# Weight transfers issued by ScalarE, fewer transfers of v, and one attention level on TensorE for two segments

## The chip, the cores and the metric

The kernel runs on one core of one Trainium2 chip. The metric is the device time in microseconds of one execution; for the kernel before, the median of 3 runs is 972.37 us (972.09 to 973.37). A profile is taken of one further execution.

## What is computed

A gated linear attention over 4 batches, 8 heads, 768 tokens and a head dimension of 48 gives a matrix of 3072 x 384. It goes through two layers of matrix products, one after the other:

```python
f = 1.0 / (1.0 + np.exp(-f_logit))
for t in range(S):
    state = f[:, :, t, :, None] * state + np.einsum('bhd,bhe->bhde', k[:, :, t], v[:, :, t])
    y[:, :, t] = np.einsum('bhd,bhde->bhe', q[:, :, t], state)
x = y.transpose(0, 2, 1, 3).reshape(B * S, H * D)
x = ((x @ w_a) * (x @ w_b)) @ w_out
h = np.maximum(np.maximum(x @ w1, x @ w2), x @ w3)
out = h @ w_out2
```

w_a and w_b are 384 x 1536, w_out 1536 x 384, w1 to w3 384 x 768 and w_out2 768 x 384. The weights arrive as float64.

## The kernel before

The 3072 tokens are cut into 12 segments of 256 tokens, three to a batch. In each segment 128 partitions hold the tokens of 8 heads; within a segment tokens are combined in levels of doubling width.

For a segment, SP loads q, k, f and v (`load_nat`, L182, two transfers each), a second layout of v called `vst` (`load_vst`, L194, 8 transfers), and from it the level operands `vlev` (`load_vlev`: segment 0 straight from `vst`, L207, 28 transfers; later segments by way of DRAM, `store_vscr` L199 and L213, 2 and 12 transfers). `direct_steps` (L229 to L283) does the levels of width 1, 2 and 4 inside blocks of 8 tokens, as elementwise multiplications and reductions: L229 to L232 width 1, L237 to L241 width 2, L248, L260, L276, L281, L282 and L283 width 4. It writes the products of decays `tp` (L257), the keys and queries `kp` and `qp` and the result so far, `op`. `attn_steps` then transposes these on TensorE (L304; ScalarE copies the results from PSUM: `c_tot` L312, `kt` and `qt` L337), builds decay tables on VectorE (L320 to L329), multiplies state and tokens (L366, L394), and does the levels of width 8, 16 and 32 as scores (L407), a mask on VectorE (L412) and a product with `vlev` (L424). `c_out` (L429) copies the segment's result, and SP transfers carry it to `xf` (L440), the input of the first MoE layer.

That layer splits every operand in a high and a low fp32r part, so that each product is three matmuls: x into `xh` (ScalarE L490) and `xl` (VectorE L493), products with w_a and w_b into `pa` and `pb` (L502), their product `a` (L512) split in `gh` (L516) and `gl` (L521), products with w_out (L531). The second layer follows in six blocks of 512 tokens (`up2` L675, `down` L701).

Weights are converted from float64 by integer and float steps in `conv_steps`, 36 units of 128 x 384 for the first layer: two activations on ScalarE (L573, L574), one step on VectorE (L579), one on GpSimd (L583), a cast on ScalarE to the high part (L590), and the low part (L595) on VectorE or GpSimd. SP issues their loads (`load_w1`, L613, and L609 for w_out).

All engines run their instructions in order. The string `ORDER` sets that order: every step is queued under a letter, and each letter of the string takes the next step of that queue. Steps called `flex` run on VectorE unless their number is in `ON_POOL`, which sends them to GpSimd. DMAs take eight completion lanes in turn, and a transfer waits for the one eight before it.

The diff touches all of `ORDER` and `ON_POOL`, the loads, `direct_steps`, `attn_steps`, `conv_steps` and the places of the second layer's buffers.

Of the kernel before, what the change touches and what calls it, by code (L numbers as in the profile page):

```python
# [7 lines left out]
F32 = mybir.dt.float32  # L8
# [35 lines left out]
    "ooGMNouMXNMuMHuoooNuoNMuoMoMuNouoMNooOuMoopOMuONuuXOMNoMouMGXoHoNuMoNMuXMuGuuNooHoNMooMoGuMoNMoXoHoN"
    "uMuMuNoMNuuoMpMGoNuoGMouooOouOYNMMNuXuouMXoNMOMouOouNoMNouMuMooNoHNMuMuoMouooNuuuMoGNHoXMHMooNuuMouX"
    "pNMoMouoNMoOouuGoONMoMOuNuMoHNOuMMGoNooMoooNuHuMMuNuuMoouoNMMuXuooNuXMoGNuXHMMoooNMNuouMXMuoooNMNuuo"
    "ouMOMoNuOouMNoOooMMONouuNMXuoMMXuNMouooNouMMoooNMouooNuMMuNouNMuooMMNooMoXOXoXoOoXOXOX"
# [30 lines left out]
def kernel(  # L78
# [31 lines left out]
    NB2 = NT // TB  # L110
    mm = nc.tensor.matmul
# [3 lines left out]
    vscr = [dram.tile([SEG, 2, 4 * D], F32, name=f"vscr{s}") for s in range(NSEG)]  # L115
# [32 lines left out]
    masks = cst.tile([P, 3, 64], U8, name="masks")  # L148
# [10 lines left out]
    tp = at.tile([P, 2, 64], F32, name="tp")  # L159
    vst = at.tile([P, 2, 2, 4, D], F32, name="vst")  # L160
    vlev = at.tile([P, 3, 2, 4 * D], F32, name="vlev")
    qt = at.tile([P, 128, 8], F32, name="qt")
# [24 lines left out]
    def load_vst(s):  # L187
        b, s0 = s // SPB, (s % SPB) * SEG
        for g in range(2):
            t0 = s0 + g * P  # L190
            for half in range(2):
                for hp in range(2):
                    h0 = 4 * hp + (half ^ hp)
                    sp.dma_start(out=vst[:, g, half, 2 * hp:2 * hp + 2],  # L194
                                 in_=v[b, h0:h0 + 3:2, t0:t0 + P, :].rearrange("h p d -> p h d"))

    def store_vscr(s):
        for g in range(2):
            sp.dma_start(out=vscr[s][g * P:(g + 1) * P], in_=vst[:, g].rearrange("p a h d -> p a (h d)"))  # L199

    def load_vlev(s):
        for lev in range(3):
            w = 8 << lev
            for hl in range(2):
                if s == 0:
                    for x in range(64 // w):
                        sp.dma_start(  # L207
                            out=vlev[64 * hl + x * w:64 * hl + (x + 1) * w, lev],
                            in_=vst[2 * x * w:2 * x * w + w, :, hl].rearrange("p g h d -> p g (h d)"),
                        )  # L210
# [603 lines left out]
```

## Time and profile before

| what | value |
| --- | --- |
| runs, median (lowest to highest) | 972.37 us (972.09 to 973.37) |
| the profiled execution | 973.67 us, span 971.9 us |
| TensorE matmul busy | 905.5 us (93%) |
| VectorE, ScalarE, GpSimd busy | 572.9, 336.1, 305.0 us |
| DMA | 79.07 MB, 81 GB/s in the mean |

The span is the profiled part of that execution; 1.8 us lie around it. TensorE carries the matmuls, VectorE is DVE in the rows, ScalarE ACT, GpSimd POOL, and SPq the DMA queue of SP. A busy share is a mean over stages with different limits; the rows further down are cut by stage.

### The profile page before, as it was taken

To read this page: it belongs to the slowest core of one execution; us is meant where nothing else is said; L and a number is where in the kernel's file an instruction comes from. 1 tells how busy PE (TensorE), PEld (TensorE's weight loads), DVE (VectorE), ACT (ScalarE), POOL (GpSimd) and SP (SyncE) were. 2 spreads that over 40 slices of the span, in tenths; PEclk is the share of its full clock that TensorE was granted. 3 is DMA by queue.
4 is the path that set the end of the run, shared out by engine and by line. 5 is a ranking of instruction groups with operands and counts; after the bars stand their busy time and mean duration, and the time that the engine had idled before them with its cause. 6 is when DMAs were issued, how large, how long until landed. Compare 5 with 4: busy or idle time off the path is not lost.

```text
span 971.9 us, 23339 instructions
## 1 busy us (share of the span) xinstructions
PE 905.5 (93%) x9860; PEld 839.5 (86%) x9860; DVE 572.9 (59%) x893; ACT 336.1 (35%) x640; POOL 305.0 (31%) x297
## 2 busy tenths in 40 slices
PE   1348989999999999999999999999999999999998
PEld 0238879999999999999999999999888888888887
DVE  6989988978886947677865442464522232323221
ACT  3556733423333333242332323564421212112121
POOL 3533737474364336443263300362400000000000
PEclk9998989999999999999999999999999999999999
DMA  8468232334323231133321204261110110010000
GB/s 244 121 198 259 79 98 59 107 76 114 106 70 93 71 115 53 58 95 83 98 84 41 69 9 137 92 212 66 33 37 17 44 49 17 33 34 17 1 32 33
DMA packets 79184, 79.07 MB, mean 81 GB/s; under 512 B 33128, under 2 KB 69864, under 8 KB 79080
## 3 DMA queue, kind: packets, MB, share of 16 engines
q1 hardware_dynamic: 79080, 77.59, 27.1%
q8 instruction: 77, 1.26, 0.5%
q14 instruction: 27, 0.22, 0.1%
HBM read 58.48 MB, written 13.76 MB: 74 GB/s over the span
## 4 chain that ended last, share of the span: by engine, by line
PE 82%; DVE 6%; DMA 6%; SPq 3%; issue 1%; ACT 1%; POOL 0%; DVEq 0%; ACTq 0%
PE p L675 23%; PE pb L502 15%; PE y L531 14%; PE pa L502 14%; PE y L701 4%; DMA ub<-in_moe_w_b_dram 2%; PE pa L701 2%; PE pb L701 2%; DMA kn<-in_k_dram 2%; PE o L424 2%; PE w L304 2%; PE o L394 2%; SPq L440 1%; PE w L407 1%; PE w L366 1%
## 5 line engine op out<-in xcount | busy, mean ns | idle before, releaser
L502 PE MATMUL pa<-xh,ua 128*128 128x256 f32 x864 | 167.7, 290 | 0.0
L502 PE MATMUL pb<-xh,ub 128*128 128x256 f32 x864 | 166.4, 288 | 1.4 <-DVE ub L595 0.9
L531 PE MATMUL y<-gh,uo 128*128 128x256 f32 x864 | 164.7, 286 | 1.5 <-ACT gh L516 0.9
L675 PE MATMUL p<-ub,u 128*128 128x512 f32 x486 | 165.9, 395 | 0.0
L502 PEld LDWEIGHTS pa<-xh,ua 128*128 128x128 f32 x864 | 137.3, 196 | 2.2
L502 PEld LDWEIGHTS pb<-xh,ub 128*128 128x128 f32 x864 | 135.2, 192 | 4.4 <-DVE ub L595 1.3
L531 PEld LDWEIGHTS y<-gh,uo 128*128 128x128 f32 x864 | 135.9, 193 | 3.4 <-ACT gh L516 1.1
L502 PE MATMUL pa<-xl,ua 128*128 128x256 f32 x432 | 124.0, 287 | 2.1 <-DVE xl L493 2.1
L531 PE MATMUL y<-gl,uo 128*128 128x256 f32 x432 | 123.4, 286 | 2.5 <-DVE gl L521 2.5
L502 PE MATMUL pb<-xl,ub 128*128 128x256 f32 x432 | 122.5, 284 | 0.0
L675 PEld LDWEIGHTS p<-ub,u 128*128 128x128 f32 x486 | 90.5, 188 | 19.1
L675 PE MATMUL p<-ua,u 128*128 128x512 f32 x324 | 101.8, 395 | 0.0
L516 ACT CAST gh<-a 128x512 fp32r<-128x512 f32 x72 | 44.6, 620 | 139.9 <-DVE a L512 118.9
L512 DVE TENSOR_TENSOR a<-a,pb 128x512 f32<-128x512 f32 x72 | 49.1, 683 | 73.2 <-PE pb L502 71.4
L502 PEld LDWEIGHTS pa<-xl,ua 128*128 128x128 f32 x432 | 84.4, 195 | 2.8 <-DVE xl L493 2.7
L531 PEld LDWEIGHTS y<-gl,uo 128*128 128x128 f32 x432 | 83.5, 193 | 3.1 <-DVE gl L521 3.1
L685 DVE TENSOR_TENSOR uo<-uo,p 128x512 f32<-128x512 f32 x36 | 24.7, 687 | 101.1 <-PE p L675 84.0
L502 PEld LDWEIGHTS pb<-xl,ub 128*128 128x128 f32 x432 | 83.1, 192 | 0.0
L508 ACT COPY a<-pa 128x512 f32<-128x512 f32 x72 | 42.5, 590 | 88.0 <-DVE gl L521 43.9
L521 DVE TENSOR_TENSOR gl<-a,gh 128x512 fp32r<-128x512 f32 x72 | 64.1, 891 | 12.8 <-ACT gh L516 12.7
L675 PEld LDWEIGHTS p<-ua,u 128*128 128x128 f32 x324 | 60.4, 188 | 11.7
L685 DVE TENSOR_TENSOR ua<-ua,p 128x512 f32<-128x512 f32 x36 | 24.8, 688 | 72.1 <-PE p L675 72.0
(206 smaller groups left out, 1560.0 us busy)
## 6 DMA issues: line engine op xcount, KB each, us to landing
u<-in_moe_w_dram SPq DMA_DIRECT2D x18, 384.0 KB
vlev<-vscr SPq DMA_DIRECT2D x132, 48.0 KB
uo<-in_moe_w_out_dram SPq DMA_DIRECT2D x14, 384.0 KB
qn<-in_q_dram SPq DMA_DIRECT2D x24, 192.0 KB
fn<-in_f_logit_dram SPq DMA_DIRECT2D x24, 192.0 KB
kn<-in_k_dram SPq DMA_DIRECT2D x24, 192.0 KB
ua<-in_moe_w_a_dram SPq DMA_DIRECT2D x12, 384.0 KB
vn<-in_v_dram SPq DMA_DIRECT2D x24, 192.0 KB
```

Of the source, the lines that this page charges most:

```text
L304: mm(pair[0][h], lhsT=pair[1][h], rhs=ident[half(h), half(h)], is_transpose=True, start=first_of_bank(n), stop=True, skip_group_check=True)
L394: mm(os_[0][64 * hl:64 * hl + D, hi // 2, o:o + 64], lhsT=st[64 * hl:64 * hl + D, c, hi * D:hi * D + D], rhs=qv[64 * hl:64 * hl + D, hi, c ...
L424: mm(ov[64 * hl:64 * hl + D, :, 1, :], lhsT=vlev[ps, lev, g, hi * D:hi * D + D], rhs=abs_[g][ps, hi, 64 * lev:64 * lev + 64], start=False, ...
L502: mm(ps, lhsT=col(w, i, j, h), rhs=x2[x][:, i], start=(n == 0), stop=(n == 3 * KC - 1), skip_group_check=True)
L508: act.copy(out=g2[jj][0], in_=ps2["a"])
L512: vec.tensor_mul(out=a, in0=a, in1=ps2["b"])
L516: act.copy(out=g2[jj][1], in_=g2[jj][0])
L521: vec.tensor_sub(out=g2[jj][2], in0=a, in1=gh.bitcast(F32))
L531: mm(ps, lhsT=wts["o", j][:, w, m * P:m * P + P], rhs=g, start=(j == 0 and n == 0 and m != 1), stop=(j == NJ - 1 and n == 2), skip_group_c ...
L675: mm(ps, lhsT=col(n, i, f, w), rhs=y, start=(c == 0), stop=(c == 3 * KC - 1))
L685: vec.tensor_max(out=hset[k][0], in0=hset[k][0], in1=u_ps[b, f, n])
L701: mm(o_ps[t], lhsT=h[:, t * P:t * P + P], rhs=wts[down_units[f]][:, w], start=(f == 0 and n == 0), stop=(f == NF - 1 and n == 2))
```

## The change

All 36 weight loads of the first layer are issued by ScalarE. Three units of one column group share one raw tile and one result tile, and `conv_steps` runs three units through its first three steps before it casts any of them. `vst` comes in 4 transfers instead of 8, goes to DRAM in 3, in all segments, and `vlev` comes in 6. For segments 0 and 1 (`DEEP = 2`) the level of width 4 leaves `direct_steps`: its scores, mask and product become `p_sc4` (L423), `mask4` (L428) and `p_av4` (L440), with two more `vlev` transfers (into a part of `prod`), the two halves of the decays kept apart in `t4`, their product `tt` formed on VectorE (L481), and the keys and queries multiplied by `t4` afterwards (L491, L492). `ORDER` and `ON_POOL` are written anew, and the second layer's buffers are cut from the new groups.

```diff
 def load_vst(s):
-            for half in range(2):
-                for hp in range(2):
-                    h0 = 4 * hp + (half ^ hp)
-                    sp.dma_start(out=vst[:, g, half, 2 * hp:2 * hp + 2],
-                                 in_=v[b, h0:h0 + 3:2, t0:t0 + P, :].rearrange("h p d -> p h d"))
+            for par in range(2):
+                sp.dma_start(out=vst[:, par, g], in_=v[b, par::2, t0:t0 + P, :].rearrange("h p d -> p h d"))
 def store_vscr(s):
-        for g in range(2):
-            sp.dma_start(out=vscr[s][g * P:(g + 1) * P], in_=vst[:, g].rearrange("p a h d -> p a (h d)"))
+        sp.dma_start(out=vscr[s][:, :, :, 0:2 * D].rearrange("p a g x -> p (a g) x"),
+                     in_=vst[:, :, :, 0:2].rearrange("p a g h d -> p (a g) (h d)"))
+        for a in range(2):
+            sp.dma_start(out=vscr[s][:, a, :, 2 * D:4 * D], in_=vst[:, 1 - a, :, 2:4].rearrange("p g h d -> p g (h d)"))
 def load_vlev(s):
-        for lev in range(3):
-            w = 8 << lev
+        for lev in range(-1 if s < DEEP else 0, 3):
+            w = 8 << lev if lev >= 0 else 4
             for hl in range(2):
...
+                sp.dma_start(
+                    out=(vlev[:, lev] if lev >= 0 else vlev4)[64 * hl:64 * hl + 64].rearrange("p g d -> p (g d)"),
+                    in_=vscr[s][:, hl].rearrange("(x two r) g d -> two x r (g d)", two=2, r=w)[0],
+                )
 def direct_steps(s):
-        for h in range(2):
+        for h in range(0 if s < DEEP else 2):
             flex("d", lambda e, h=h: e.tensor_mul(
...
+        if s < DEEP:
+            step("c", lambda: act.copy(out=tp[:, :, :, 0:D], in_=t4v.rearrange("p h two d -> p two h d")))
+            step("c", lambda: act.copy(out=kpv[:, :, :, 0:D], in_=hh(kn)))
+            step("c", lambda: act.copy(out=qpv[:, :, :, 0:D], in_=hh(qn)))
+        else:
...
+        if s < DEEP:
+            return
 def attn_steps(s):
+        def p_sc4():
+            w = ws["4"] = banks(ps_w, "w").rearrange("p h (i x) -> p h i x", i=2)
...
+        def mask4():
+            ab = abs_[4] = abp.tile([P, 4, 3 * 64], F32, tag="ab", name="ab")
...
+        def p_av4():
...
         step("b", c_tr, qt)
+        if deep:
+            step("b", lambda: act.copy(out=k8.rearrange("p x r -> p (x r)").rearrange("p (x r) -> p x r", r=4), in_=kt[:, :, 0:4]))
+            step("P", p_sc4)
+            step("h", mask4)
+            flex("h", lambda e: e.tensor_mul(out=kt[:, :, 0:4], in0=kt[:, :, 0:4], in1=_bc(t4[:, 1].rearrange("p a b -> p (a b)"), 2, 4)))
+            flex("h", lambda e: e.tensor_mul(out=qt[:, :, 4:8], in0=qt[:, :, 4:8], in1=_bc(t4[:, 0].rearrange("p a b -> p (a b)"), 2, 4)))
+            step("P", p_av4)
 def conv_steps(kinds, units, done):
+        for n0 in range(0, len(units), KC):
+            for n in range(n0, n0 + KC):
+                for kind, f in zip(kinds, (s1, s2, s3)):
+                    step(kind, f, n)
+            for n in range(n0, n0 + KC):
+                step(kinds[3], s4, n)
+                flex(kinds[4], lambda e, n=n: s5(n, e))
 def load_w1(n, c, i):
...
-        sp.dma_start(out=dst, in_=w[i * P:(i + 1) * P, 2 * c * DM:2 * (c + 1) * DM])
+        act.dma_start(out=g[:, i].rearrange("p c t -> p (c t)"), in_=src[i * P:(i + 1) * P])
```

The new table of orders shows best on three queues. The names are as in the text above; a row is a line of the kernel, an operation, what it writes and reads, the shape, and how often.

SP's queue from the loads of segment 0's `vlev` to the first transfer of segment 0's result (`xf`), before:

```order
L207 DMA vlev<-vst 8x2x192 x16
L207 DMA vlev<-vst 16x2x192 x8
L207 DMA vlev<-vst 32x2x192 x4
L613 DMA ub_479<-in_moe_w_b_dram 128x768
L613 DMA ub_488<-in_moe_w_b_dram 128x768
L182 DMA vn<-in_v_dram 64x2x384 x2
L609 DMA uo_560<-in_moe_w_out_dram 128x768
L194 DMA vst<-in_v_dram 128x2x48 x8
L440 DMA xf<-k64n 48x256 x2
```

and with the change:

```order
L199 DMA vscr_57<-vst 512x1x96
L202 DMA vscr_57<-vst 128x2x96 x2
L208 DMA prod<-vscr_57 64x1x384 x2
L208 DMA vlev<-vscr_57 64x1x384 x6
L186 DMA vn<-in_v_dram 64x2x384 x2
L196 DMA vst<-in_v_dram 128x4x48 x4
L473 DMA xf<-k64n 48x256 x2
```

The weight loads are gone from SP, and 28 transfers have become 3 to DRAM and 8 back.

TensorE from the last products of segment 0 to the first products of the first MoE layer (`pa`), before:

```order
L424 MATMUL o<-ab,vlev 48x8x8 x8
L424 MATMUL o<-ab,vlev 48x4x16 x8
L424 MATMUL o<-ab,vlev 48x2x32 x8
L304 MATMUL o<-ident,tp 128x64 x2
L304 MATMUL w<-ident,kp 128x64 x16
L304 MATMUL w<-ident,qp 128x64 x16
L502 MATMUL pa<-xh,ua_225 128x256 x2
L502 MATMUL pa<-xl,ua_225 128x256
```

and with the change:

```order
L457 MATMUL o<-ab,vlev 48x8x8 x8
L457 MATMUL o<-ab,vlev 48x4x16 x8
L457 MATMUL o<-ab,vlev 48x2x32 x8
L307 MATMUL o<-ident,tp 128x64 x4
L307 MATMUL w<-ident,kp 128x64 x16
L307 MATMUL w<-ident,qp 128x64 x16
L307 MATMUL o<-ident,op 128x32x2 x16
L423 MATMUL w<-qt,k_125 64x64 x16
L545 MATMUL pa<-xh,ua_254 128x256 x2
L545 MATMUL pa<-xl,ua_254 128x256
```

The transposes of `op` and `p_sc4` of segment 1 (L307 of `op`, L423) now stand ahead of the first product; before, those of `op` stood 24 rows behind it.

ScalarE from segment 0's `c_out` (into `k64n`), before:

```order
L429 COPY k64n<-o 128x1024
L590 CAST ua_642<-cvt 128x384
L476 COPY st<-st 128x192
L573 ACTIVATE cvt<-ub_479 128x384
L574 ACTIVATE ub_479<-ub_479 128x384
L573 ACTIVATE cvt<-ub_488 128x384
L574 ACTIVATE ub_488<-ub_488 128x384
L255 COPY kp<-kn 128x2x4x48
L590 CAST ua_668<-cvt 128x384
L490 CAST xh<-xf 128x256
L312 COPY tt<-o 128x2x32x2
L590 CAST ub_694<-cvt 128x384
```

and with the change:

```order
L462 COPY k64n<-o 128x1024
L519 COPY st<-st 128x192
L616 ACTIVATE cvt<-uo_529 128x384
L617 ACTIVATE uo_529<-uo_529 128x384
L317 COPY t_120<-o 128x2x32x2
L633 CAST ub_693<-cvt 128x384
L317 COPY t_120<-o 128x2x32x2
L655 DMA ua_697<-in_moe_w_a_dram 128x768
L633 CAST ub_693<-cvt 128x384
L655 DMA ua_697<-in_moe_w_a_dram 128x768
L633 CAST ub_693<-cvt 128x384
```

The tables' copies of segment 1 (`t_120`, L317) come four rows after `c_out`, and weight transfers stand between the casts.

## Rows read from the trace of the kernel before

**Rows 1.** The windows view, five stretches: length, busy us per engine (instructions), granted clock, DMA share, GB/s.

```profile
0.00:69.40 69.40, 19.00 (x404) 16.31 (x404) 57.24 (x103) 32.82 (x66) 31.00 (x29) 1.00 0.66 183
69.40:97.20 27.80, 22.28 (x211) 20.76 (x210) 25.90 (x56) 17.06 (x37) 7.52 (x7) 0.88 0.87 262
97.20:121.50 24.30, 22.73 (x393) 21.31 (x391) 24.23 (x39) 19.24 (x42) 17.33 (x13) 1.00 0.27 79
121.50:145.80 24.30, 20.54 (x160) 19.14 (x161) 21.28 (x36) 9.67 (x22) 8.03 (x10) 0.86 0.37 98
145.80:947.60 801.80, 800.44 (x8602) 744.28 (x8601) 439.41 (x657) 252.95 (x471) 241.12 (x239) 1.00 0.23 67
```

**Rows 2.** The windows view again, two stretches cut at VectorE's first instruction and at TensorE's first product.

```profile
8.90:69.40 60.50, 19.00 (x404) 16.31 (x404) 57.19 (x102) 30.49 (x63) 28.70 (x18) 1.00 0.65 181
69.40:136.70 67.30, 56.45 (x676) 52.65 (x675) 65.33 (x119) 41.92 (x89) 30.43 (x23) 0.92 0.51 149
```

**Rows 3.** The waits of TensorE, 0 to 146 us: total, times, longest.

```profile
PE o L304 <- DVE tp L257: 28.6, 2, 20.0
PE o L304 <- DVE op L283: 8.2, 2, 4.8
```

**Rows 4.** The timeline of TensorE around the first products, and again near 134 us.

```profile
65.87 0.37 PE L304 MATMUL o<-ident,tp 64*128 64x64 f32 x2 [8.67 <-DVE tp L257]
...
69.41 0.79 PE L502 MATMUL pa<-xh,ua 128*128 128x256 f32 x2
...
78.61 0.40 PE L502 MATMUL pb<-xh,ub 128*128 128x256 f32 x2
...
79.41 0.47 PE L304 MATMUL o<-ident,op 64*128 64x64 f32 x8
...
133.74 0.58 PE L531 MATMUL y<-gl,uo 128*128 128x256 f32 x1 [1.50 <-DVE gl L521]
134.12 0.63 PE L531 MATMUL y<-gh,uo 128*128 128x256 f32 x2
...
139.93 0.40 PE L502 MATMUL pa<-xh,ua 128*128 128x256 f32 x2
```

**Rows 5.** The timeline of VectorE, segments 0 and 1.

```profile
8.95 0.96 DVE L229 TENSOR_TENSOR prod<-qn,kn 128x768 f32<-128x768 f32 x1 [8.09 <-DMA kn<-in_k_dram]
10.00 0.96 DVE L230 TENSOR_TENSOR qn<-qn,fn 128x768 f32<-128x768 f32 x1
...
45.09 1.65 DVE L230 TENSOR_TENSOR qn<-qn,fn 128x768 f32<-128x768 f32 x1
...
54.65 0.96 DVE L412 TENSOR_TENSOR ab<-w,masks 128x768 f32<-128x768 f32 x1 [1.12 <-PE w L407]
```

**Rows 6.** The timeline of GpSimd beside the third row of rows 5.

```profile
44.42 1.50 POOL L583 TENSOR_TENSOR cvt<-cvt,uo 128x384 int32<-128x384 int32 x1 [1.19 <-ACT cvt L573]
```

**Rows 7.** VectorE's groups by form up to 69.4 us: busy, mean ns.

```profile
L248 DVE TENSOR_TENSOR prod<-qn,kn 128x768 f32<-128x768 f32 x4 | 4.4, 1146 | 0.0
L260 DVE TENSOR_REDUCE sc<-prod 128x32 f32<-128x1536 f32 x2 | 3.5, 1736 | 0.0
...
L237 DVE TENSOR_TENSOR prod<-qn,kn 128x384 f32<-128x384 f32 x4 | 2.1, 547 | 0.0
...
L454 DVE TENSOR_TENSOR k<-kt,gt 128x512 f32<-128x512 f32 x1 | 0.7, 676 | 0.0
```

**Rows 8.** The timeline of ScalarE, from segment 0's last copy.

```profile
57.26 1.01 ACT L429 COPY k64n<-o 128x1024 f32<-128x1024 f32 x1 [1.41 <-PE o L424]
58.17 0.52 ACT L590 CAST ua<-cvt 128x384 fp32r<-128x384 f32 x1
```

**Rows 9.** The timeline of SP's DMA queue, segment 0.

```profile
10.68 5.32 SPq L194 DMA_DIRECT2D vst<-in_v_dram  x8
16.04 0.94 SPq L613 DMA_DIRECT2D ub<-in_moe_w_b_dram  x2
...
27.69 21.03 SPq L207 DMA_DIRECT2D vlev<-vst  x28
```

More of the change, by code (lines that the diff above doesn't have):

```diff
@@ L114 @@
     dram = ctx.enter_context(tc.tile_pool(name="dram", bufs=1, space=bass.MemoryType.DRAM))
-    vscr = [dram.tile([SEG, 2, 4 * D], F32, name=f"vscr{s}") for s in range(NSEG)]
+    vscr = [dram.tile([P, 2, 2, 4 * D], F32, name=f"vscr{s}") for s in range(NSEG)]
     yscr = [dram.tile([P, KC, SEG], F32, name=f"yscr{s}") for s in range(NSEG)]
@@ L292, in attn_steps @@
         first = s % SPB == 0
+        deep = s < DEEP
         ws, os_, abs_ = {}, {}, {}
@@ L308, in p_tot, with c_tot @@
             o = os_[0] = banks(ps_o, "o")
-            turn([[o[:, h, 0:64] for h in range(2)]], [[tp[half(h)].rearrange("p h d -> p (h d)") for h in range(2)]])
-        def c_tot():
-            act.copy(out=tt.rearrange("p (h i c) b -> p h (c b) i", h=2, i=2),
-                     in_=os_[0][:, :, 0:64].rearrange("p h (x i) -> p h x i", i=2))
+            n = 2 if deep else 1
+            turn([[o[:, h, 64 * a:64 * a + 64] for h in range(2)] for a in range(n)],
+                 [[tp[half(h), a].rearrange("p h d -> p (h d)") for h in range(2)] for a in range(n)])
+        def c_tot(a):
+            act.copy(out=(t4[:, a] if deep else tt).rearrange("p (h i c) b -> p h (c b) i", h=2, i=2),
+                     in_=os_[0][:, :, 64 * a:64 * a + 64].rearrange("p h (x i) -> p h x i", i=2))
         tv = tt.rearrange("p x (h b) -> p x h b", h=2)
@@ L444, in attn_steps @@
         step("P", p_tr, kp)
-        step("b", c_tot)
+        for a in range(2 if deep else 1):
+            step("b", c_tot, a)
+        if deep:
+            flex("g", lambda e: e.tensor_mul(out=tt, in0=t4[:, 0], in1=t4[:, 1]))
         tables()
@@ L564, with conv_steps @@
     SIGN = 2.0 ** 32
-    NCV = 5
-    def conv_steps(kinds, units, pool_of):
+    NCV = 4
+    def conv_steps(kinds, units, done):
         live = {}
@@ L588, in s4 @@
             del raw[u]
[L589 removed]
+            wts[u] = done(u)
             act.copy(out=wts[u][:, 0], in_=t)
@@ L622, in units1 @@
             units += [(n, c, i) for n in "ab" for i in range(KC)]
-            units += [("o", 3 * c + j) for j in range(3)]
+            units += [("o", KC * c + i) for i in range(KC)]
         return units
@@ L637, in open_w2, with spare, done2 @@
         ps_p.append(ctx.enter_context(tc.tile_pool(name="ps_p", bufs=4, space=bass.MemoryType.PSUM)))
+    def spare(n, c, dt=F32):
+        if (n, c) not in spares:
+            spares[n, c] = room(wp, (n, c), [P, KC, 2 * DM], dt)
+        return spares[n, c]
+    def done2(u):
+        if u[0] == "o":
+            return spare("o", 2, F32R)[:, u[1] % KC].rearrange("p (t c) -> p t c", t=2)
+        return room(w2p[0], u, [P, 2, DM], F32R)
     def load_w2(u):
-        pool = w2p[0]
         if u[0] == "q":
@@ L648, in load_w2 @@
             src = (w1, w2, w3)[n][i * P:(i + 1) * P, 2 * c * DM:2 * (c + 1) * DM]
-        sp.dma_start(out=raw_tile(pool, u), in_=src)
+        if u[0] == "o":
+            raw[u] = spare("b", 3)[:, u[1] % KC].bitcast(U32).rearrange("p (c t) -> p c t", t=2)
+        else:
+            raw[u] = room(w2p[0], u, [P, DM, 2], U32)
+        sp.dma_start(out=raw[u].rearrange("p c t -> p (c t)"), in_=src)
+    spares = {}
     yf, yhl, hset, o_ps, u_ps = {}, {}, {}, {}, {}
@@ L680, in rest2 @@
         if n == 0:
-            hset[k] = [room(wp, u, [P, TB], F32 if i == 0 else F32R) for i, u in
-                       enumerate([("o", 3 + i) if k == 0 else ("a", 2, i) for i in range(3)])]
+            h = spare(*(("o", 1), ("a", 2))[k], F32R)[:, :, 0:TB]
+            hset[k] = [spare("a", 3)[:, k, 0:TB], h[:, 0], h[:, 1]]
             act.copy(out=hset[k][0], in_=u_ps[b, f, n])
@@ L730 @@
     step("i", load_consts)
-    for u in units1():
-        step("r", load_w1, u)
-    conv_steps("01234", units1(), lambda u: wp)
+    for c in range(DFF // DM):
+        for n in "abo":
+            for i in range(KC):
+                step("r", load_w1, n, c, i)
+    conv_steps("01234", units1(), done1)
     for s in range(NSEG):
@@ L776, in _consts @@
     ident = np.eye(128, dtype=np.float32)
-    masks = np.zeros((128, 3, 64), np.uint8)
-    for lev in range(3):
-        w = 8 << lev
+    masks = np.zeros((128, 4, 64), np.uint8)
+    for lev in range(4):
+        w = 4 if lev == 3 else 8 << lev
         i = np.arange(64) // w
```

159 lines of the change are left out of this document (83 added, 76 removed), and 25 rows, old and new, of the table ON_POOL.

## The prediction

> **What bounds the kernel now.** I first cut the span into stretches and compared TensorE's busy time with their length [rows 1]. From 145.8 to 947.6 us TensorE is busy for 800.44 of 801.80 us at full clock: nothing that changes other engines there can win time, as long as they stay ahead. Before that, 50.4 us of the first 69.4 are idle, then 5.5, 1.6 and 3.8 us in the next three stretches (length less busy time). So all that can be won or lost lies in the first 146 us, in two amounts: T1, the moment at which the first product of the first MoE layer starts, and TensorE's idle time behind it, 10.9 us up to 145.8. TensorE's waits then say for whom it idles [rows 3]: 28.6 us twice for `tp`, 8.2 us twice for `op`, all of it work of VectorE's `direct_steps`. The longest of the two waits for `op` is 4.8 us, so the other, segment 1's, is 3.4. VectorE is busy for 57.19 of the 60.5 us between its first instruction and T1 and for 65.33 of the next 67.3 [rows 2]: it bounds the start-up, first by segment 0's chain and then by sheer volume.
>
> The timeline of TensorE shows the seam [rows 4]. T1 is 69.41 us. Segment 1's first transposes, which stand ahead of it, have waited 8.67 us for `tp` at 65.87. The first products run at 0.63 to 0.79 us a pair until about 78.2 and at 0.40 from there, that is at the lower of the clock's two levels (1.2 and 2.4 GHz) after an idle stretch. It happens again at 134: after a wait of 1.50 us for `gl` pairs take 0.63 us, and 0.40 again at 139.93.
>
> **The change, part by part.**
>
> *Two segments' width-4 level goes to TensorE.* Per deep segment VectorE loses L248 twice, L260, L276 twice and L281 (768 elements) and L256, L259, L282, L283 (384 elements). By the rows that is 2 x 1.15 + 1.74 + 3 x 0.96 + 4 x 0.55 = 9.1 us (the 0.96 is that of L230, also 768 elements) [rows 5, 7]. It gains `tt`, `mask4` and the two multiplications by `t4`, each at most 512 elements, 0.68 us: 2.4 us at most after allowing less for the small `tt`. So 6.7 us a segment, 13 us in both. ScalarE gains three fuller copies and one more turn of `t4`; I take 2 us each segment. TensorE gains 16 small products twice. For segment 0 they lie in its idle time; of segment 1 only `p_av4` falls behind T1, by the nearest row 16 products of 0.47 us per 8 (at 79.41), 0.9 us [rows 4]. In exchange segment 1's 16 transposes of `op`, which now stand behind T1, go ahead of it: the same 0.9 us back. I set both against each other.
>
> *Steps moved to GpSimd.* By the order, VectorE's rows up to segment 1's last `xl` sum to 103 us of single durations before and 83 after: 20 us less, of which 13 by the level above and the rest by steps that GpSimd takes (58 of its instructions up to there, before 41). This is no free gift: L230 took 0.96 us alone and 1.65 us beside a GpSimd conversion of 1.50 us [rows 5, 6]. Averaged over all 41 such instructions of GpSimd before, VectorE's excess over its shortest durations was about 0.45 us for each (19.5 us in all, summed over the 220 instructions of both stretches, whose busy time rows 2 give). So 17 more cost some 8 us, and the net relief is 12 us by segment 1's `xl`, not 20.
>
> The page "SBUF — State Buffer" of the Trainium skill (section "Who interferes with whom") says that a VectorE instruction with two SBUF inputs and a GpSimd instruction that reads SBUF share an exclusively locked port, so that one fully waits. The row of 1.65 us agrees in part: 0.69 of the neighbour's 1.50 us came on top, not all of it.
>
> *v in 13 transfers.* SP spent 5.32 us on issuing 8 `vst` and 21.03 us on the 28 `vlev` of segment 0 [rows 9]. After: 4 and 11 (`vscr` 3, `vlev` 8). Before, `vlev` was needed only by segment 0's last products, behind a mask that came at 54.65 [rows 5], so SP's 48.7 us was no limit; but the queue behind it (segment 1's `vn`, `vst`) came late. Now a trip through DRAM lies ahead of `vlev`. As an estimate from VectorE's first wait (the loads issued from the start on have landed at 8.95 [rows 5]) one landing takes 4 to 5 us, two take 9, and the path ends near 35 us; `p_av4` of segment 0 wants it at 35 to 40. I cost it at nothing; were it late, VectorE's `kt` would not wait, TensorE's row of `p_av4` would, with all behind it. In later segments TensorE's full stretch hides the savings.
>
> *Weights issued by ScalarE.* Two transfers cost SP 0.94 us [rows 9], so one costs ScalarE's sequencer 0.47 us, 36 of them 17 us spread over 100. A transfer also waits, in ScalarE's order, for the eighth one before it, and behind it stand PSUM copies. ScalarE is busy 30.49 of the 60.5 us ahead of T1 [rows 2], so the issue time fits. In numbers: up to T1, three transfers stand between segment 0's last copy and segment 1's tables: 1.4 us on the path.
>
> *T1.* VectorE started at 8.95 us, after a wait of 8.09 for k [rows 5]. Now a weight transfer is issued beside the first loads, and the second half of q waits for a slot: I take +1.2, bounds 0 and 3.3. Segment 0's last mask was at 54.65, that is 45.7 us after the start, of which 39.9 are durations. Now the durations are 37.3, because segment 1's direct steps are put ahead of segment 0's masks and eat most of the relief; with the same 5.8 us of waits and lengthening, and 4.3 for half of 19 more GpSimd instructions at 0.45, it comes at 10.2 + 47.4 = 57.6. The last copy `c_out` started 2.6 us after the mask (57.26) and took 1.01 [rows 8]: it ends at 61.2. Behind it ScalarE has 20 instructions and three transfers up to the `k` copy on which `p_sc4` of segment 1 waits, and TensorE's order has that row ahead of the first product. By rows 2 an instruction is 0.48 us (30.49 over 63), less 0.09 by which successive ones overlap (58.17 against 58.27 in rows 8): 7.8 us, one more for two copies of 1024 elements, 1.4 for the transfers, 0.9 for `p_sc4`, and 0.7 for a conversion that waits for GpSimd: 73.0. So T1 is **3.6 us later**. Bounds: 66 if GpSimd costs VectorE nothing and the start is not delayed, 80 if each of the three transfers waits and VectorE loses the full duration.
>
> *Behind T1.* By 73 segment 1's direct steps are all but done. VectorE reaches segment 1's `xl` some 12 us earlier than before, at about 123 instead of 134, just ahead of TensorE. Of 10.9 us of idle time the 3.4 for `op` go, most of the waits near 130 go, and some 3.7 stay (`xl` behind T1, conversions of the second column group): **-7.2**, bounds -2.9 and -9.9. Without the waits at 130 to 134 there is no second stretch at half clock; it lasted 5.5 us, in which 0.63 against 0.40 us a pair loses 0.36 of the time, about 2.0, and 2.4 with its first, single products: **-2.4**, bound 0.
>
> **Sum**: +3.6 - 7.2 - 2.4 = -6.0. The profiled execution took 973.67 us, so 967.7; it stands 1.3 us above the median of the runs (972.37), so **966.4**. The bounds: -3.4 - 9.9 - 2.4 gives 956.7; +10.6 - 2.9 gives 980.1.
>
> **The rivals.** (A) *ScalarE blocked by its own transfers: slower.* Its queue is in order, and the DMA share of 0.87 at 262 GB/s from 69.4 to 97.2 [rows 1] shows that landings are not quick just there. If two of the transfers ahead of T1 stand some 6 us each on the eighth one before, `c_tot`, `kt` and `c_out` come 12 us later, T1 is 85, later work is further along (idle 1 less than in my case): 972.4 + 15.6 - 8.2 - 2.4 + 3.0 for a longer stretch at half clock = 980. It decides from about T1 = 79, where +9.6 cancels -9.6. For it: in-order queue, three weight transfers in six ScalarE rows ahead of `k64n`. Against: ScalarE has 30 us to spare. (B) *No change.* If GpSimd takes as much from VectorE as it takes over (17 instructions at 1.2 us instead of 0.45, 20 us), `xl` of segment 1 is late as before: -3.4 for `op` alone, +3.6 for T1: 972.6. The rule of an exclusive port, above, would make it so. (C) *The relief comes whole*: T1 66, idle 3: 972.4 - 3.4 - 7.9 - 2.4 = 958.7. (D) *The transfers don't move.* If the 16 engines' bandwidth and not SP's issuing sets when weights land (0.87), they land no earlier, the conversions stay late, and TensorE keeps the waits near 130: +3.6 for T1, -3.4 for `op`, -2.4 for the stretch at half clock at best, 970.2 to 972.6.
>
> The page "DMA: Bandwidth & Descriptors" of the Trainium skill (section "Issuing engines are not separate DMA queues") says that transfers of several engines run on the same 16 engines and that only issue time is saved. By it (D) is what the first part gives; no row so far separates the two.
>
> **How the numbers follow.** A measurement here tells some 0.2%, 1.9 us, from no change. My case 0.46; A 0.22; B and D 0.12, of which 0.09 within 0.2%; C 0.20. Faster by over 0.2%: 0.45 + 0.20 + 0.03 = 0.68; within 0.10; slower 0.22. The range 957 to 979 leaves out the far end of C (0.06) and half of A (0.11).
>
> **What would show it.** TensorE's first product between 70 and 76 us; VectorE's wait for `kn` or `qn` ending near 10; segment 0's second mask near 58; idle time of TensorE from T1 to 145.8 below 5 us and no pair of 0.63 us near 134; the busy time behind 145.8 unchanged. I am wrong if ScalarE's transfers wait several us ahead of a copy on the chain (A), if GpSimd's and VectorE's instructions lengthen so that segment 1's `xl` is past 130 (B), or if idle time appears behind 146 us, which no row of before suggests.

## The result and the profile after

The changed kernel takes **984.52 us** (median of 4 runs, 983.2 to 985.81), the kernel before 972.49 us beside it: a ratio of 1.0122, interval 1.0105 to 1.014. It is 12 us slower; 966.4 us was forecast, with a range up to 979. The profiled execution took 984.87 us, its span 983.1.

The windows view of the changed kernel, cut at its first MoE product and then as rows 1 (columns as there):

```profile
0.00:78.80 78.80, 22.99 (x520) 19.84 (x520) 58.75 (x98) 41.57 (x83) 40.92 (x50) 1.00 0.68 182
78.80:97.20 18.40, 15.24 (x148) 14.71 (x143) 14.42 (x24) 9.04 (x19) 5.05 (x6) 0.91 0.67 176
97.20:121.50 24.30, 19.85 (x311) 19.15 (x313) 18.07 (x35) 13.69 (x29) 9.26 (x7) 0.86 0.68 210
121.50:145.80 24.30, 23.35 (x309) 22.24 (x300) 23.81 (x40) 16.71 (x36) 10.56 (x10) 1.00 0.28 70
145.80:960.00 814.20, 807.75 (x8632) 750.87 (x8632) 444.22 (x673) 253.72 (x473) 238.69 (x232) 1.00 0.23 67
```

T1 is 78.85 us instead of 69.41. Length less busy time is 55.8 us ahead of it (50.4 before), then 3.2, 4.4 and 1.0, together 8.6 us up to 145.8 (10.9 before), and 6.5 us from there to 960 (1.4 before, up to 947.6). Against [rows 1], TensorE idles 5.4 us more ahead of T1 and 2.5 us more behind it, and is busy 4.0 us more ahead of T1 and 0.7 us less behind: the span is 11.2 us longer.

TensorE's waits of the changed kernel, 0 to 160 us (total, times, longest), show other names than [rows 3]:

```profile
PE o L307 <- ACT tp L251: 21.1, 1, 21.1
PE w L307 <- DVE kt L498: 8.3, 1, 8.3
PE o L307 <- POOL op L271: 6.0, 2, 4.7
PE w L371 <- ACT k64n L361: 5.6, 2, 3.7
...
PE o L440 <- DMA prod<-vscr: 4.5, 2, 3.7
PE pa L545 <- ACT a L551: 3.2, 1, 3.2
```

Two of them hold a long wait that is new, each for a copy of ScalarE: 3.7 us for `k64n` and 3.2 us for `a`. The wait for `prod` is that of segment 0's `p_av4` for the trip through DRAM, at 36 us; TensorE then idles 8.3 us more for `kt` of VectorE, so it held nothing up. ScalarE's timeline shows what held the two copies (ACTq is ScalarE's issuing; in brackets idle time and releaser):

```profile
39.89 0.33 ACTq L655 DMA_DIRECT2D ua<-in_moe_w_a_dram  x1
40.27 0.55 ACT L616 ACTIVATE cvt<-uo 128x384 f32<-128x384 f32 x1 [3.10 <-DMA vlev<-vscr]
...
82.84 0.33 ACTq L655 DMA_DIRECT2D ub<-in_moe_w_b_dram  x1
83.22 0.55 ACT L616 ACTIVATE cvt<-ua 128x384 f32<-128x384 f32 x1 [5.20 <-DMA prod<-vscr]
...
86.65 0.56 ACT L551 COPY a<-pa 128x512 f32<-128x512 f32 x1
...
100.19 0.33 ACTq L655 DMA_DIRECT2D uo<-in_moe_w_out_dram  x1
100.57 1.01 ACT L361 COPY k64n<-w 128x1024 f32<-128x1024 f32 x1 [5.35 <-DMA qn<-in_q_dram]
```

The instructions that idle read neither `vscr` nor `qn`. What waits is the weight transfer just ahead of them in ScalarE's order: its completion lane, the one eight transfers back, was last taken by a transfer that **SP** had issued, and that one came late. SP's queue around the second and third case:

```profile
74.18 0.59 SPq L199 DMA_DIRECT2D vscr<-vst  x1
74.82 2.55 SPq L202 DMA_DIRECT2D vscr<-vst  x2
79.74 1.24 SPq L208 DMA_DIRECT2D prod<-vscr  x2
...
88.71 1.88 SPq L186 DMA_DIRECT2D qn<-in_q_dram  x2
```

SP reads `vscr` back only after its stores have landed, at 79.74; the last packets of that read landed at 82.82, ScalarE issues its weights at 82.84, and the copy `a` behind it starts at 86.65. In the third case SP's transfer was not issued late but was long under way: SP issued `qn` from 88.71 on, and the weights that wait for its lane were issued at 100.19, 11.5 us later. TensorE's timeline is the other end of the chain:

```profile
78.85 0.79 PE L545 MATMUL pa<-xh,ua 128*128 128x256 f32 x2
...
87.27 0.80 PE L545 MATMUL pa<-xh,ua 128*128 128x256 f32 x2 [3.16 <-ACT a L551]
...
89.99 0.63 PE L545 MATMUL pa<-xh,ua 128*128 128x256 f32 x2
...
90.63 0.42 PE L545 MATMUL pa<-xh,ua 128*128 128x256 f32 x2
```

After 3.16 us of idling pairs of products take 0.63 us, 0.4 again from 90.63, as in [rows 4] at 134: the granted clock of that stretch is 0.91, and 0.86 in the next, where TensorE waited 3.66 us for `k64n`.

VectorE's timeline, segment 0:

```profile
11.75 0.96 DVE L224 TENSOR_TENSOR prod<-qn,kn 128x768 f32<-128x768 f32 x1 [6.33 <-DMA qn<-in_q_dram]
...
45.70 1.21 DVE L498 TENSOR_TENSOR kt<-kt,gt 128x1024 f32<-128x1024 f32 x1
...
60.17 0.96 DVE L445 TENSOR_TENSOR ab<-w,masks 128x768 f32<-128x768 f32 x1 [0.38 <-PE w L412]
...
64.06 0.96 DVE L445 TENSOR_TENSOR ab<-w,masks 128x768 f32<-128x768 f32 x1 [1.53 <-PE w L412]
```

VectorE starts 2.8 us later than before and reaches the second mask 52.3 us after its start; before it was 45.7 [rows 5].

### The profile page after: what moved, and what is told of

Read it like the earlier page. It is cut to its first block, busy times and chain, and to the rows that moved or that the text cites. A ratio compares the mean times of both kernels' runs of the same rounds, so it can differ in the third digit from the quotient of the medians.

```text
span 983.1 us, 23425 instructions
## 1 busy us (share of the span) xinstructions
PE 908.8 (92%) x9992; PEld 844.0 (86%) x9992; DVE 563.6 (57%) x872; ACT 339.1 (34%) x646; POOL 304.5 (31%) x304
## 4 chain that ended last, share of the span: by engine, by line
PE 74%; DVE 11%; DMA 6%; SPq 3%; issue 2%; ACT 2%; POOL 1%; ACTq 0%; DVEq 0%; POOLq 0%
PE p L738 23%; PE y L574 12%; PE pb L545 12%; PE pa L545 12%; PE y L764 4%; DMA qn<-in_q_dram 2%; PE pb L764 2%; PE pa L764 2%; PE o L457 2%; PE w L412 2%; SPq L473 2%; PE o L399 1%; PE w L307 1%; DMA vscr<-vst 1%; PE w L371 1%
## 5 line engine op out<-in xcount | busy, mean ns | idle before, releaser
L748 DVE TENSOR_TENSOR ua<-ua,p 128x512 f32<-128x512 f32 x72 | 49.5, 687 | 155.4 <-PE p L738 155.4
L738 PEld LDWEIGHTS p<-ua,u 128*128 128x128 f32 x324 | 60.5, 188 | 11.4
L738 PE MATMUL p<-uo,u 128*128 128x512 f32 x162 | 64.1, 396 | 0.0
```

What stands on the lines that cost most here:

```text
L738: mm(ps, lhsT=col(n, i, f, w), rhs=y, start=(c == 0), stop=(c == 3 * KC - 1))
L748: vec.tensor_max(out=hset[k][0], in0=hset[k][0], in1=u_ps[b, f, n])
```

## The experiments

Ratios are to the kernel before, measured beside each run, with their 95% intervals.

**e1.** The weights are issued by SP again, all else as changed.

```diff
-        act.dma_start(out=g[:, i].rearrange("p c t -> p (c t)"), in_=src[i * P:(i + 1) * P])
+        sp.dma_start(out=g[:, i].rearrange("p c t -> p (c t)"), in_=src[i * P:(i + 1) * P])
```

> The changed kernel (984.5 us) with one word undone: the 36 weight transfers are issued by SP again, at the same places of the order. Theory Q (ScalarE's in-order queue stands at transfers whose slot is still held by one of SP's transfers, at 39.9, 83.2 and 100.2 us): ScalarE's waits for DMA of 5.2 and 5.3 us behind the first product go, TensorE's waits for the copies a (3.2) and k64n (3.7) go with the half-clock stretches behind them, 8 to 10 us: 974 to 977. Theory P (GpSimd's added instructions lengthen VectorE's) and theory S (the first weight transfers delay q): nothing changes but the 0.4 us an issue, 982 to 985. If SP's queue becomes the new bound (36 more issues of 0.47 us ahead of vlev and xf), slower: 988 or more.

Measured: 976.57 us, 1.0036 (1.0022 to 1.0049). So 8 of the 12 us come from the issuing by ScalarE. None of ScalarE's three stalls above is left, and none for `vscr` or `qn` is in its waits. The windows, cut at T1 (76.07) and as above:

```profile
0.00:76.00 76.00, 22.61 (x520) 19.70 (x520) 58.98 (x98) 41.77 (x85) 40.96 (x50) 1.00 0.65 183
76.00:97.20 21.20, 20.43 (x247) 19.48 (x239) 16.94 (x32) 11.94 (x25) 7.76 (x8) 1.00 0.78 221
97.20:121.50 24.30, 20.24 (x374) 19.15 (x374) 23.44 (x41) 17.74 (x38) 12.14 (x10) 1.00 0.51 175
```

The granted clock is full in all three, and there are 0.8 us of idle time between T1 and 97.2 where the changed kernel has 3.2. Still T1 stays 6.7 us later than before.

**e2.** As changed, with 19 of GpSimd's steps back on VectorE.

The edit takes the numbers 1, 9, 11, 40, 52, 53, 54, 57, 62, 87, 89, 92, 95, 97, 100 and 102 to 105 out of `ON_POOL`.

> The changed kernel with 18 steps of segments 0 and 1 and of the first conversions back from GpSimd on VectorE; GpSimd keeps its two steps at the start and the third conversion step. Theory P: VectorE's excess over its shortest durations from its start to segment 0's second mask falls from 13 to about 5 us while it gains 2.7 us of work there, so that mask comes 5 us earlier (59 instead of 64), the first product near 74; total 978 to 981. Theories Q and S: VectorE only has more to do, the first product 3 us later than 78.9, total 985 to 989.

Measured: 983.83 us, 1.0116 (1.0098 to 1.0133). VectorE's lengthening (busy time over the shortest duration of each form) from its start to the second mask fell from 13.2 to 9.1 us, but it had that much more to do: moving steps to GpSimd wins as much as it loses.

**e3.** As changed, with q, k, f and v loaded ahead of the first weights, and the first conversion steps moved behind them (the lines are cut at the right).

```diff
-    "rjkzz0qrr1czddddvdddd0rd2di0t...
+    "jkqzzvr0rrczdddd1dddd0rd2di0t...
```

> The changed kernel with the first three weight transfers behind the loads of f, k, q and v in the order (and the first two conversion steps on VectorE behind the first attention steps). Theory S: VectorE's first instruction at 9 instead of 11.75 us, everything up to the first product 2.5 us earlier, total 981 to 983. Against it: if bandwidth as such is the limit there, the start stays at 11 to 12 and the total at 984 to 986, later conversions included.

Measured: 980.2 us, 1.0085 (1.0063 to 1.0106); VectorE starts at 9.75. So the edit gives back some 4 of the 8 us, but not by the start alone, where ScalarE's two transfers of 384 KB lie beside SP's `qn`: T1 (77.15) is only 1.7 us earlier. The stall at 39.9 is gone, and the granted clock from 78.8 to 97.2 is 1.00 instead of 0.91; the stalls of 4.4 us for `vscr` and 5.2 for `qn` are still there. The two edits overlap, so this is no share of the 8.

**e4.** The kernel before with its weights issued by ScalarE.

```diff
-        sp.dma_start(out=dst, in_=w[i * P:(i + 1) * P, 2 * c * DM:2 * (c + 1) * DM])
+        act.dma_start(out=dst, in_=w[i * P:(i + 1) * P, 2 * c * DM:2 * (c + 1) * DM])
... (and the same for w_out)
```

> The kernel before (972.4 us) with one part of the change alone: the weight transfers issued by ScalarE, at the same places of the old order. Theory Q: ScalarE stands behind slots held by SP's transfers, above all by the 28 vlev transfers of segment 0 (27.7 to 48.7 us), copies for TensorE come late: 976 to 985. Theories P and S: the first weights come earlier, nothing else moves: 970 to 974.

Measured: 975.55 us, 1.0028 (1.0017 to 1.0038): slower there too, by 2.4 us. ScalarE's timeline has the same kind of stall:

```profile
87.78 0.33 ACTq L613 DMA_DIRECT2D ub<-in_moe_w_b_dram  x1
88.22 0.56 ACT L573 ACTIVATE cvt<-ua 128x384 f32<-128x384 f32 x1 [4.30 <-DMA vlev<-vscr]
```

**e12.** The first 18 weight transfers by ScalarE, the last 18 by SP.

```diff
-        act.dma_start(out=g[:, i].rearrange("p c t -> p (c t)"), in_=src[i * P:(i + 1) * P])
+        (act if c < 2 else sp).dma_start(out=g[:, i].rearrange("p c t -> p (c t)"), in_=src[i * P:(i + 1) * P])
```

> The changed kernel with the first 18 weight transfers on ScalarE as changed and the last 18 on SP. Theory Q in two parts: the late start of q (2.5 to 2.8 us) belongs to the first transfers and stays, first product at 78.5 to 79; the stalls of 5.2 and 5.3 us belong to the last ones and go, with the half-clock stretches: total 978 to 980. If it were the issuing as such, half of the 8 us: 980 to 981; if SP then blocks, 984 and more.

Measured: 977.76 us, 1.0055 (1.0036 to 1.0074). T1 is 79.48, no better than in the changed kernel, yet 6.8 us are back, and no wait of ScalarE for `vscr`, `vlev` or `qn` is left: they were lost by the last 18 transfers, behind T1. And T1 3.4 us later than in e1 costs 1.2 us in the end: a later T1 is partly made good behind it.

**e5, e6, e11, e8.** Segment 1's direct steps are put behind segment 0's masks (18 letters moved): e5 as changed, e6 with weights on SP, e11 as e6 with the copies L251 and L252 behind `c_out`, e8 as e6 with e2's steps back. The edit of e5:

```diff
-...Vg0d2rPhhh13344c3dg014drr2d02b1d2lPhd3b03ghrddh14hdvh01rP34g4drb2Ph2rh0bh1hddh23hhtPh0drd3r14dPhPc04dP30dhrcP2bP1b1x
+...Vg02rPhhh13344c3g014rr202b12lPh3b03ghrh14hvh01rP34g4rb2Ph2rh0bhd1hhd23hhtPhdd0r3r14PddhdddP04P30hddddddcddrcP2bP1b1x
```

> The changed kernel with 18 letters of its order moved: the 17 direct steps of segment 1 (and one copy) that stand ahead of segment 0's scaled keys, state updates and masks go behind them or into their waits; everything else, ScalarE's transfers included, as it is. Theory O (the new order puts segment 1's steps ahead of the chain on which the first product hangs: kt, the state, the masks, the copy of segment 0's result, its transfers to xf): that copy starts at about 60 instead of 66.7 us, the first product at about 72 instead of 78.9, total 977 to 980, less only if the stalls of ScalarE behind the first product shrink too. Against it (VectorE's volume sets the first product, as segment 1's tables stand ahead of it): the first product stays at 77 to 79, total 983 to 985.

> The same move of letters with the weight transfers on SP (the kernel of the run that had 976.6 us). Theories O and Q together: the first product at 69 to 70, no stall of ScalarE on a transfer behind it, total 969 to 971, below the kernel before (973). If VectorE's volume behind the first product takes it back (segment 1's steps are now late), idle time appears between 90 and 140 us, total 974 to 977.

> The kernel of the second run of this set with the 19 steps of segments 0 and 1 back from GpSimd on VectorE. Theory P (GpSimd's instructions cost VectorE as much as they take over): within 1.5 us of that run, either way. If they were worth something now that the order no longer hides it: 3 us slower or more; if they cost more than they give: 3 us faster.

> The kernel with the weights on SP and segment 1's direct steps behind segment 0's masks, as in the earlier run of 977.1, but with ScalarE's two copies for segment 1's first transposes behind segment 0's last copy instead of ahead of it (there it had waited 4.1 us for a GpSimd step). Theory O: that last copy at 61 instead of 64.9, the first product at 73 to 75, total 972 to 974. If VectorE's volume sets the first product: it stays at 77 to 80, total 976 to 978.

Measured: e5 988.59 us, 1.0154 (1.014 to 1.0168); e6 977.08, 1.0036 (1.0024 to 1.0049); e8 976.64, 1.0033 (1.0021 to 1.0045); e11 976.12, 1.0037 (1.0023 to 1.005). On SP the order of masks and direct steps makes no difference; with ScalarE's issuing (e5) it costs 4 us. In e11 `c_out` started at 62.6, in e6 at 64.9 and in e1 at 64.2, and T1 was 80.4, 80.0 and 76.1: an earlier `c_out` did not bring T1 forward, since segment 1's tables, `op` and `p_sc4`, which TensorE's order has ahead of the first product, then end last. My idea that the place of the masks sets T1 fell; two chains end together there.

**e7.** The kernel before with v's new transfers only (a part of the edit).

```diff
-                    sp.dma_start(out=vst[:, g, half, 2 * hp:2 * hp + 2],
+                sp.dma_start(out=vst[:, par, g], in_=v[b, par::2, t0:t0 + P, :].rearrange("h p d -> p h d"))
...
```

> The kernel before with the v part alone: 4 transfers of vst, 3 to DRAM (also for segment 0), 6 of vlev; the order is the old one with one letter more. My forecast costed this at nothing: 971.5 to 973.5. If SP's 28 issues had held up segment 1's loads and weights: 968 to 971. If the trip through DRAM makes vlev of segment 0 late (its last products wait behind 52 us): 975 or more.

Measured: 972.24 us beside 973.31, 0.9988 (0.9979 to 0.9997): a gain of 1.1 us.

**e9, e10.** As changed, and as e1, with the width-4 level of both segments back on VectorE, its steps put where before has them.

```diff
-    DEEP = 2
+    DEEP = 0
... (ORDER and ON_POOL to match)
```

> The changed kernel with DEEP = 0: segments 0 and 1 do their width-4 level on VectorE again, in the order otherwise kept (13 steps a segment back, 11 out). My forecast took the level on TensorE for 13 us of VectorE's time: without it the first product would come 5 to 8 us later than 78.9 and the total be 988 to 994. Theory C (the level on TensorE puts a round trip of ScalarE, TensorE, the mask and two multiplications into the chain ahead of kt and so gives back what VectorE saves): first product within 3 us of 78.9, total 982 to 987.

> The same with the weight transfers on SP (beside the kernel with 976.6 us and the first product at 76.1). By my forecast's term 981 to 986, the first product at 81 to 84; by theory C 975 to 979.

Measured: e9 987.73 us, 1.0155 (1.0138 to 1.0172), 3.2 us above the changed kernel; e10 985.66, 1.0135 (1.012 to 1.015), 9.1 above e1. T1 moved by 13.0 us (78.85 to 91.84) and 13.1 (76.07 to 89.18).

**e13, e14, e15.** e10 takes the level out of an order made for it. These put it into the order of before: weights on SP, conversion and order of before, v's new transfers, and the level on TensorE for both segments (e13, e14) or for segment 0 alone (e15). In e13 the small table of segments 2 and later lies in columns that a later step overwrites, so from segment 2 on e13 does not compute the result; e14 gives the table a buffer of its own.

```diff
+    DEEP = 2
-    "zqzjckzrd0drd0vdddirdddr1tddddrddrcd0dP1drr12br2ddgd3Pgcd2b3kP4jgbd0hdgdgr13dg020dgdd4qd1ggdhbrrd01b"
+    "zqzjckzrd0drd0vdddirdddr1tddddrrcc0P1rr12bbgr2dgd3Pgcd2b3kP4jgbbd0dgdgr13dg0V20dgPPhhhh4lq1gghbrr01b"
...
```

> The kernel of before with its own order, its own conversion by single blocks and its weights on SP, and of the change only two parts: v's transfers as in e7, and the first two segments' last direct level on TensorE (the new steps put in at the places where before had the ones that go; tp lies in op's first columns and the small table of the level in q32, since the storage is short). Theory N (the new order and the conversion in threes give back what the level brings; before with the level alone is better than before): before 972.5, less 1.1 for v (e7), less some 9 for the level (e10 against e1 was worth 9.1), some of it lost since the steps are put in by hand: 960 to 968; first MoE product before 62. Rival M (the level on TensorE brings nothing in before's order: its 132 products more and its longer chain of kt, qt, scores and mask eat what VectorE gains, and e9 and e10 only show an order that was made for it being run without it): 970 to 976, with the first MoE product at 66 to 72. Rival L (the chain ahead of the first product gets longer): above 976.

> As e13 (old order, old conversion, weights on SP, v's transfers as in the change, the last direct level of segments 0 and 1 on TensorE), with a buffer of its own for the small table of segments 2 and later, which in e13 lay in columns that a later step overwrote. Same instructions, so the time of e13: 968 to 971, that is 2.5 to 5 us below before, with the first MoE product at 66 to 67. That is theory M with a rest: the level is worth some 2 to 3 us to the whole in before's order, not 9. If it is above 972.5, e13's gain came from the shared columns and the level is worth nothing here.

> e14 with the level on TensorE for segment 0 alone; segment 1 keeps its products on VectorE, where MoE products of segment 0 already run. Theory A (only what lies ahead of the first product counts, so segment 1's level is worth nothing or costs its 66 products, some 2 us of TensorE): first product at 66 to 67, whole 967 to 969, below e14. Theory B (VectorE limits segment 1 too, as the idle stretches of 69 to 137 us in before show): 970 to 972.5, above e14 by 1 to 3.

Measured: e13 969.4 us, 0.9959 (0.9945 to 0.9972); e14, in a later session, 971.51 beside 973.05, 0.9989 (0.998 to 0.9998); e15 972.84, 0.9995 (0.9985 to 1.0006). The windows of e14, cut at its T1 (65.39):

```profile
0.00:65.30 65.30, 20.95 (x472) 18.11 (x472) 48.29 (x96) 35.40 (x71) 30.00 (x29) 1.00 0.68 193
65.30:97.20 31.90, 26.07 (x301) 24.50 (x298) 25.21 (x55) 19.53 (x41) 10.07 (x9) 0.95 0.96 291
97.20:121.50 24.30, 22.42 (x389) 20.96 (x388) 24.30 (x39) 18.34 (x39) 15.98 (x12) 1.00 0.14 41
121.50:145.80 24.30, 20.83 (x176) 19.48 (x175) 22.24 (x35) 10.67 (x22) 9.37 (x12) 0.93 0.38 98
```

VectorE is busy 48.29 us up to T1 instead of 57.24 [rows 1], and T1 is 4.0 us earlier (e7, with v's part alone: 0.8 us). The profiled execution keeps 3.4 us of that in its span; the medians, with v's part of 1.1 us in them, show 1.5 us less. By e14's ratio against e7's, 0.9989 and 0.9988, the level alone is worth nothing that the runs can tell, give or take 1.2 us by the two intervals. e13's ratio would give it 2.8 us, but e13 does not compute the result, so it prices nothing. It is not the 9 us of e10 in any case. e14 and e15 do not settle segment 0 against 1: their intervals overlap.

## Why the prediction was wrong, step by step

**"Weights issued by ScalarE ... so the issue time fits"** is the step that failed. I priced a transfer at 0.47 us of issuing and took three of them, 1.4 us; the issuing itself took 0.33 us in the rows above. I had written that a transfer waits for the eighth before it, but put no price on it, as if only weights stood in that row. The lanes are shared with SP's transfers, of which some stand behind data (`vscr`) and some take long to land (`qn`); one of them late is a stall for all of ScalarE. e1, which gives 8 us back, has none of the three stalls of 3.10, 5.20 and 5.35 us nor the lower clock after the last two; it also starts VectorE 2.5 us earlier, which is nearly all of the 2.8 us by which its T1 is earlier. How the 8 us divide between stalls and start is only bounded: e12 puts 6.8 behind T1. That is rival A's sign and its kind, with another cause and place: A had two stalls of 6 us ahead of T1, by ScalarE's own transfers; two of the three lie behind T1, and all three are by SP's transfers.

**The forecast of T1, 73.0**, was 78.85. By its own parts: start 11.75 for 10.2 (2.8 us later than before, inside the bound of 3.3); from the start to the second mask 52.3 us for 47.4; from the mask to `c_out` 2.6, as said; from `c_out`'s end to T1 11.2 for 11.8. The long part is VectorE's stretch: less the 37.3 us of durations, 15.0 us of waits and lengthening for the 10.1 assumed, and 13.2 of lengthening alone. But e2 cut that to 9.1 and won nothing, and e11 brought `c_out` forward by 2.3 us against e6 and won nothing: the sum followed one chain where two end together. T1 is 5.8 of the 17.2 us by which the span missed the forecast; 11.4 lie behind it.

**"Behind T1 -7.2"**: idle time up to 145.8 fell by 2.3 us only, and 5.1 us came behind 145.8, where I had none. The waits near 134 did go, as said; ScalarE's stalls and new waits took their place. e1 has the later ones too (1.9 us of idle time from 150 to 200 us and 3.5 from there to 600, 0.6 and 0 before), so they are not ScalarE's issuing. From 200 to 600 us the windows of before, e14, e1 and e10, in this order, show whose they are:

```profile
200.00:600.00 400.00, 400.00 (x5942) 388.17 (x5942) 271.06 (x418) 130.11 (x232) 165.23 (x170) 1.00 0.27 76
200.00:600.00 400.00, 400.00 (x5942) 388.18 (x5941) 269.12 (x412) 130.74 (x233) 163.80 (x169) 1.00 0.28 77
200.00:600.00 400.00, 396.47 (x5788) 384.40 (x5778) 265.50 (x404) 128.61 (x232) 168.84 (x172) 1.00 0.26 71
200.00:600.00 400.00, 395.83 (x5771) 383.37 (x5771) 270.79 (x417) 129.27 (x234) 175.63 (x176) 1.00 0.27 74
```

With the order of before TensorE does not idle there, with v's transfers and the level on TensorE (e14) or without; with the new order it idles 3.5 us and more, with the level on TensorE (e1) or back on VectorE (e10). No weight is converted between 150 and 600 us, so the conversion in threes is not it either: what is left is the new order itself with its `ON_POOL`. One wait, of 2.8 us in the changed kernel:

```profile
480.29 0.96 DVE L261 TENSOR_TENSOR op<-vn,sc 128x768 f32<-128x768 f32 x1 [3.63 <-DMA vn<-in_v_dram]
481.17 1.32 DVE L564 TENSOR_TENSOR gl<-a,gh 128x512 fp32r<-128x512 f32 x1
...
483.21 0.80 PE L545 MATMUL pa<-xh,ua 128*128 128x256 f32 x2 [2.80 <-ACT a L551]
```

VectorE's next attention step waits for a late `vn` with the MoE's `gl` queued behind it, ScalarE's copy `a` behind that, and TensorE's products behind the copy. To move that load alone was not tried.

**"The lower clock -2.4"**: the stretch at 134 went, two new ones came up to 145.8 and short ones later (0.63 us a pair again behind the wait at 483); busy time behind T1 fell by 0.7 us. In e1, without the first two, it fell by 4.5.

**The level on TensorE**: 13 us less work for VectorE was near (up to T1 e10's VectorE is busy 70.2 us, e1's 59.0); what it is worth in the end was not. In the order of before VectorE does 9 us less up to T1 and T1 moves by some 3 more than v alone moves it, of which the runs keep nothing that they can tell.

**v at nothing**: it gains 1.1 us (e7). **GpSimd's 8 us of harm against as much relief**: a wash, as rival B has it (e2 0.7 us, e8 0.4). The count of GpSimd's instructions does not tell the harm: up to the second mask VectorE is lengthened by 13.2 us beside 25 of them, in e2 by 9.1 beside 15. Nearly all of it falls on instructions that run beside one of GpSimd's. Three pairs of the changed kernel show its size:

```profile
16.39 1.32 POOL L626 TENSOR_TENSOR cvt<-cvt,ua 128x384 int32<-128x384 int32 x1
16.77 1.36 DVE L232 TENSOR_TENSOR prod<-qn,kn 128x384 f32<-128x384 f32 x1
...
27.45 1.18 POOL L626 TENSOR_TENSOR cvt<-cvt,ub 128x384 int32<-128x384 int32 x1
27.68 1.03 DVE L327 TENSOR_TENSOR ft<-tt 128x32 f32<-128x32 f32 x1
...
57.76 0.94 POOL L262 TENSOR_TENSOR prod<-vn,sc 128x384 f32<-128x384 f32 x1
58.32 1.20 DVE L261 TENSOR_TENSOR op<-vn,sc 128x768 f32<-128x768 f32 x1
```

GpSimd's instruction had 0.94, 0.95 and 0.38 us left when VectorE's began; VectorE's took 0.82, 0.82 and 0.25 us more than its shortest of that form (0.54, 0.20 and 0.95). So it lost all but 0.13 us of what was left, whatever its own size. L383, which reads PSUM, took its usual 0.35 us at 58.05 beside the same GpSimd instruction as L261. The page "SBUF — State Buffer" of the Trainium skill (section "Who interferes with whom") has an exclusive lock there, and these rows agree with it. The row of 1.65 us in the prediction does too: I set its 0.69 us against the neighbour's whole 1.50, but only 0.83 of them were left when it began [rows 5, 6].

**Rival D**, that the transfers don't land earlier: the DMA share from T1 to 97.2 is 0.67 where it was 0.87 [rows 1], so in the mean the engines had room. But `qn` took up to 11.5 us to land from 88.71 on, which the runs do not explain, so D stays open. The page "DMA: Bandwidth & Descriptors" (section "Issuing engines are not separate DMA queues" of the Trainium skill) says that only time on the issuing sequencer is saved. The runs show the other half: it is spent on the sequencer that gets the transfers, with the waits.

The account of the 12 us, then: some 8 for ScalarE's issuing (984.52 less 976.57). e1 still lies 3.5 us above before, though v gains 1.1. Its profiled execution, 1.8 us below e1's median, has a span 1.1 us longer than that of before: idle time is 3.0 us more ahead of T1, 5.2 less from there to 145.8 and 4.1 more behind 145.8, and busy time 0.8 less. So the second step that failed is that TensorE's full stretch would stay full: without the idle time behind 145.8, which comes with the new order, e1 would be no slower than before. How much of the later T1 (+6.7 us in e1) belongs to the order, with segment 1's direct steps, its `op` and its `p_sc4` ahead of the first product, and how much to the conversion in threes was not tried apart and stays open. Of the kernels that compute all of it the fastest are e14 and e7, with before's order: 0.1% below before.

## What to carry to other kernels

Before DMAs are moved to a compute engine's queue, list for each what holds its completion slot, across all queues that share the slots; issue time is the small part, and the engine stands still for a late transfer of any neighbour. Price a saving on an engine by the moment that ends last behind it, in the order in which it will run: VectorE lost 9 us of work up to T1 in e14, and the kernel won nothing that the runs can tell. Where two chains end together, shortening one wins nothing, and a mark like "the first product" says little about the end: it came 3.4 us later in e12 than in e1 for 1.2 us of time.

## What the runs showed of the hardware that was not expected

An encounter with GpSimd cost a VectorE instruction of 32 elements as much as one of 384, 0.82 us in the rows above, because the loss follows what is left of GpSimd's instruction and not VectorE's own length. So steps of VectorE's tables of 32 elements, 0.20 us each alone, took up to 1.03 us.

And two 384-KB transfers of ScalarE, issued from 4.49 us on beside SP's `qn` (issued from 3.53), came with a late landing of `qn`: VectorE began at 11.75 us. With those weights issued by SP it began at 9.26; with q, k and f first, and ScalarE's two issued at 4.99 and 5.74, at 9.75.
